# Three half chunks of a convolution's input gradient with leaf C by three products, twin sums in one instruction, and raw step buffers kept free of pair sums

## The chip, the core and the metric

The kernel runs on one core of one Trainium2 chip. The time is that of one launch on the device, in microseconds (us); the kernel before has three runs, and their median is what a new time is held against. One further execution was taken with the hardware profiler; every duration, wait and share below is of that execution. Its span goes from the first to the last recorded instruction.

## The reference, cut to what matters

A strided one-dimensional convolution (31 taps, stride 2, 256 channels to 256), a normalisation over time, a GELU, and the gradients of all of it.

```python
B, T, D, K = 2, 16000, 256, 31                      # x: (B, T, D), w: (K, D, D), all bf16
L = (T - K) // 2 + 1                                # 7985
h = sum(einsum('blc,cd->bld', x[:, i:i + 2*L:2, :], w[i]) for i in range(K))
h = (h - mean(h)) / sqrt(var(h) + 1e-5)             # over l, for each b and d
out = gelu(h * gn_gamma + gn_beta)
# returned: out, and the gradients of x, w, gn_gamma, gn_beta for a given grad_out (B, L, D)
```

The matmuls are those of three convolutions: the forward one, the one that gives the gradient of x, and the one that gives the gradient of w.

## The kernel before, in words

**Fewer products for sums.** Each convolution is split by even and odd positions, twice, and each split is done with three products in place of four: from the parts e0 and e1 of the data the kernel forms sums (the branches A, C and B of the first split, the leaves A, C and B of the second), multiplies each with a matching difference of weights, and adds the results with signs. A leaf can be done directly (helpers `f_leaf`, `g_leaf`, `w_leaf`) or split a third time. In the input gradient a direct leaf is 16 matmuls of 512 columns (`g_leaf`: two output parities, four positions, two channel halves). Split a third time it is 12: four by `g_three_b` or `g_outer` for the product that both parities share, and eight by `g_three_ac` on the sums of the two planes, which are formed by the function `third`. The shared product then has to be brought to both parities with opposite signs, which is work for VectorE (DVE) or ScalarE (ACT), in `g_seed`.

**Stages.** F0 and F1 are the forward pass of batch 0 and 1 (matmuls of line 596), G0 and G1 the input gradient (line 1162; G1 begins with the last chunk of batch 0), W the weight gradient (line 1447). GELU and its gradient (`gelu_unit`, lines 943 to 983) for batch 0 run beside F1, for batch 1 beside G0. The input gradient goes over two batches b, four chunks c, two half chunks pr, and the branches in the order B, A, C. In `input_grad` (line 1279) `GO` names the steps whose leaf A is split a third time (all of batch 1), and `GOC` the half chunks (b, c, pr) whose leaf C is too: the set is empty. Four PSUM tiles of two banks each are the ring in which a step's two results px and pt are built; before a leaf may add into its tile, `g_seed` (line 1202) must have written the signed results of the branch before into it, on DVE.

**Sums on DVE.** `third` and half of `second` add a plane to the other plane, and the other plane to the first one shifted by one element: always two instructions (lines 561 and 1121, through the local `tt`). In the weight gradient `pair_d` (line 1511) forms two differences of four rows each with two instructions at line 1516; `pair_x` (line 1504) is line 1508, `leaf_d` line 1587.

**The weight gradient's buffers.** `weight_grad` (line 1575) goes over nine steps n (`COMBOS`, line 22). For each, `x_tile` (line 1417) loads four blocks of x from HBM (1 MB each) into the tiles XS_ or XT_, by turns; where the step needs the sum of two raw blocks, the second is loaded into one of two raw buffers XR (byte 57344 and byte 65536 of the arena) and added by DVE (`w_add`, line 1413). Steps 2, 3, 5 and 6 need raw sums, the loads standing at the end of the step before. The pair sums of a step lie in sets named by `place` (line 1578): "all", "early" (steps 0 and 1) and "late", and the set "late" lies on the bytes of XR. Before, "late" is open to all steps but 3 and 5, by turns; step 4 puts the pair sums of its middle leaf there.

**The order.** Nothing of the order is written by hand. Each operation is recorded with an estimated duration; `Plan.order` (line 170) derives due times from the place of its readers among the matmuls, moved by a table of leads for each stage and kind of operation, and `Plan.listing` walks the engines and picks the most urgent ready operation. TensorE may take an operation up to `look` places ahead of the recorded order, and the result is pinned.

## Time and profile before

| what | value |
|---|---|
| runs | 1188.23, 1187.01, 1183.07 us; median 1187.01 us |
| profiled execution | 1189.54 us, of which the span is 1187.8 us |
| TensorE (PE) busy | 1149.0 us, 97% of the span |
| DVE busy | 1047.6 us, 88% |
| ACT busy | 570.0 us, 48% |
| granted TensorE clock, mean | 0.996 |
| forward matmuls (line 596) end | about 429 us |
| input gradient's matmuls (line 1162) | about 426 to 861 us |
| weight gradient's matmuls (line 1447) | about 861 us to the end |

The page of the profile gives, for each engine, busy time, and for each group of instructions "busy, mean ns of one | idle time of the engine before them and what ended it". [...] PEclk is the granted TensorE clock as a share of full speed.

### The profile page before, as it was taken

The numbers are of one execution on the slowest core, as the hardware profiler recorded it, in microseconds if no ns is written. First come the engines' busy times: TensorE is split into PE (matmuls) and PEld (weight loads), VectorE is DVE, ScalarE is ACT, GpSimd is POOL, SyncE is SP. The second block draws the span as 40 slices with busy tenths as digits, with TensorE's granted clock in tenths as the row PEclk, the third lists the DMA queues.
The fourth block names the chain that finished last, engine by engine and source line by source line (L and its number), as shares of the span: only waits on it lengthen the run. The fifth ranks groups of instructions, "written<-read, shape, count | busy, mean of one in ns | idle before, by whom it ended". The sixth has DMA issues, their size and how long they took to land.

```text
span 1187.8 us, 19338 instructions
## 1 busy us (share of the span) xinstructions
PE 1149.0 (97%) x7739; PEld 763.5 (64%) x7796; DVE 1047.6 (88%) x1358; ACT 570.0 (48%) x873; POOL 18.9 (2%) x67
## 2 busy tenths in 40 slices
PE   5999999999999999999999999999999999989998
PEld 3888889777777964444444444444488656656685
DVE  7997898799999989999879997788889898777995
ACT  1254454788885578978884476433322212111200
POOL 0000000000000000000000000000000000000000
PEclk9999999999999999999999999999999999999999
DMA  9446949968986799567639998697998824986774
GB/s 212 73 115 122 200 121 182 205 146 204 204 209 124 270 353 252 167 225 186 221 115 292 270 329 265 161 318 266 317 235 266 271 90 151 359 300 198 239 219 140
DMA packets 334100, 255.17 MB, mean 215 GB/s; under 512 B 187500, under 2 KB 312682, under 8 KB 325738
## 3 DMA queue, kind: packets, MB, share of 16 engines
q1 hardware_dynamic: 333818, 253.93, 76.6%
q8 instruction: 61, 1.00, 0.3%
q14 instruction: 29, 0.24, 0.1%
q0 software_dynamic: 192, 0.00, 0.0%
HBM read 118.95 MB, written 89.62 MB: 176 GB/s over the span
## 4 chain that ended last, share of the span: by engine, by line
PE 46%; DVE 14%; DMA 6%; issue 4%; ACT 1%; SPq 0%; DVEq 0%; ACTq 0%
PE ps L1162 27%; PE ps L1447 15%; PE ps L596 4%; DVE arena L1413 3%; DMA arena<-in_x_dram 2%; DMA arena<-dnd 2%; DVE arena L1357 2%; DVE arena L1587 2%; DVE ps L676 1%; DVE arena L676 1%; DVE arena L1516 1%; DVE arena L1508 1%; DMA dnd<-arena 1%; DVE arena L1121 1%; DVE ps L1540 1%
## 5 line engine op out<-in xcount | busy, mean ns | idle before, releaser
L1162 PE MATMUL ps<-arena 128*128 128x512 bf16 x1974 | 429.7, 376 | 6.6 <-DVE ps L676 3.6
L596 PE MATMUL ps<-arena 128*128 128x256 bf16 (+4 forms) x3460 | 408.2, 281 | 17.8 <-DVE arena L551 7.1
L596 PEld LDWEIGHTS <-arena 128*128 128x128 bf16 x3460 | 338.1, 99 | 87.7 <-DVE arena L551 7.5
L1162 PEld LDWEIGHTS <-arena 128*128 128x128 bf16 x2016 | 197.3, 98 | 237.7 <-issue 6.8
L1447 PE MATMUL ps<-arena 128*128 128x256 bf16 (+1 forms) x2305 | 312.1, 298 | 10.5 <-DVE arena L1508 7.3
L1447 PEld LDWEIGHTS <-arena 128*128 128x128 bf16 x2320 | 228.1, 98 | 94.6 <-DVE arena L1508 8.7
L691 ACT ACTIVATE arena<-ps 128x1024 f32<-128x1024 f32 (+1 forms) x143 | 145.7, 1020 | 285.3 <-PE ps L1447 98.1
L561 DVE TENSOR_TENSOR arena<-arena 128x1087 bf16<-128x1087 bf16 (+3 forms) x211 | 175.5, 866 | 13.7 <-PE ps L596 12.4
L968 DVE TENSOR_TENSOR arena<-arena 128x1024 bf16<-128x1024 bf16 x160 | 107.0, 683 | 8.5 <-ACT arena L962 3.9
L1413 DVE TENSOR_TENSOR arena<-arena 128x4096 bf16<-128x4096 bf16 x38 | 86.3, 2284 | 20.8 <-DMA arena<-in_x_dram 19.5
L1121 DVE TENSOR_TENSOR arena<-arena 128x516 bf16<-128x516 bf16 (+3 forms) x176 | 83.6, 506 | 8.6 <-PE ps L1162 8.0
L676 DVE TENSOR_TENSOR ps<-ps,arena 128x1024 f32<-128x1024 f32 x60 | 73.1, 1224 | 7.9 <-PE ps L1447 4.5
L1357 DVE TENSOR_TENSOR arena<-arena 128x768 bf16<-128x768 bf16 (+3 forms) x112 | 65.4, 636 | 9.9 <-DMA arena<-dnd 4.7
L711 ACT ACTIVATE arena<-ps 128x512 bf16<-128x512 f32 (+1 forms) x64 | 36.9, 578 | 70.4 <-PE ps L596 67.9
L676 DVE TENSOR_TENSOR ps<-arena,ps 128x1024 f32<-128x1024 f32 x44 | 53.8, 1223 | 9.3 <-PE ps L1162 5.5
L1532 ACT COPY ps<-ps 128x256 f32<-128x256 f32 x54 | 19.3, 357 | 78.7 <-PE ps L1447 77.6
L1587 DVE TENSOR_TENSOR arena<-arena 128x2304 bf16<-128x2304 bf16 x36 | 47.4, 1348 | 4.8 <-PE ps L1447 4.8
L1516 DVE TENSOR_TENSOR arena<-arena 128x1024 bf16<-128x1024 bf16 x76 | 48.7, 682 | 1.6 <-DMA arena<-d2d 1.6
L551 DVE TENSOR_TENSOR arena<-arena 128x2048 bf16<-128x2048 bf16 (+1 forms) x52 | 49.8, 989 | 0.0
L958 DVE SCALAR_TENSOR_TENSOR arena<-arena 128x1024 bf16<-128x1024 bf16 x32 | 39.0, 1219 | 11.3 <-ACT arena L956 11.1
L1189 ACT ACTIVATE ps<-ps 128x512 f32<-128x512 f32 x48 | 27.9, 582 | 41.1 <-PE ps L1162 38.0
L1508 DVE TENSOR_TENSOR arena<-arena 128x2048 bf16<-128x2048 bf16 x38 | 45.3, 1216 | 1.2 <-PE ps L1162 1.2
(79 smaller groups left out, 632.8 us busy)
## 6 DMA issues: line engine op xcount, KB each, us to landing
arena<-in_x_dram SPq DMA_DIRECT2D x40, 1024.0 KB, 9.8
arena<-d2d SPq DMA_DIRECT2D x16, 1216.0 KB, 11.5
out_dram<-arena SPq DMA_DIRECT2D x14, 1024.0 KB, 4.4
d2d<-arena SPq DMA_DIRECT2D x30, 384.0 KB, 7.1
arena<-dnd SPq DMA_DIRECT2D x10, 960.0 KB, 5.8
vl<-arena SPq DMA_DIRECT2D x36, 256.0 KB, 3.3
arena<-vl SPq DMA_DIRECT2D x9, 1024.0 KB, 6.8
hd<-arena SPq DMA_DIRECT2D x8, 1024.0 KB, 5.0
```

Source lines behind the costliest of these rows:

```text
L561: lambda: nc.vector.tensor_tensor(out=o, in0=a, in1=b, op=ALU.add))
L596: yield nc.tensor.matmul(ps[:, dh, cs], lhsT=wt, rhs=mv, start=s0, stop=False, skip_group_check=True)
L676: add("DVE", dve(1024, 1), [out], [a, b], lambda: nc.vector.tensor_tensor(out=out, in0=a, in1=b, op=op))
L691: lambda: nc.scalar.activation(out=out, in_=ps, func=ACT.Copy, scale=scale))
L968: add("DVE", dve(1024), [o], [a, b_], lambda: V.tensor_tensor(out=o, in0=a, in1=b_, op=op))
L1121: lambda: nc.vector.tensor_tensor(out=o, in0=a, in1=b, op=ALU.add))
L1162: yield nc.tensor.matmul(ps[:, e, 0:wide], lhsT=lt, rhs=mv, start=s0, stop=False, skip_group_check=True)
L1357: lambda: nc.vector.tensor_tensor(out=out, in0=a, in1=b_, op=ALU.subtract))
L1413: add("DVE", dve(4096), [o], [a, b], lambda: nc.vector.tensor_tensor(out=o, in0=a, in1=b, op=ALU.add))
L1447: yield nc.tensor.matmul(ps[:, s, c0:c1], lhsT=lt, rhs=mv, start=s0, stop=False, skip_group_check=True)
L1516: add("DVE", dve(1024), [d4[:, j]], [d], lambda j=j, o=o, st_=st_: nc.vector.tensor_tensor(out=d4[:, j], in0=d[:, o:o + 3 * st_ + 1:st_, : ...
L1587: add("DVE", dve(2304), [DL[i3, b]], [D2[b]], lambda b=b, i3=i3, o_=o_: nc.vector.tensor_tensor(out=DL[i3, b], in0=D2[b][:, o_:o_ + 17:2, ...
```

## The change

1. `GOC` is filled: leaf C of the half chunks (1, 1, 0), (1, 1, 1) and (1, 2, 0), three branches each, is split a third time. Its weight differences are formed by `w2_outer(C_)` before, and `third` runs once more for each of two chunks and three branches.
2. The two instructions of each twin sum become one. A helper `crossed` builds an access pattern whose first row is the other plane and whose second row is the first plane shifted by one element, that is, a row step of one element less than a plane, backwards. `pair_d` likewise becomes one instruction, with a negative row step. The pairs of sums in U and the last columns that are zeroed are laid out for it.
3. `place` closes the set "late" to steps 2 and 4 as well, so the raw buffers hold no pair sums from step 2 to step 5.
4. `f_first` records the first weight differences in another order, one of them after the first sum of x; `w2_part` of batch 0 is called at another branch in the first three chunks.
5. The planner's numbers are others: slack 50 in place of 70, `look` 14 in place of 13, the pads, the whole table of leads, and PACE, which spreads the GELU units.

```diff
-        self.look = 13
+        self.look = 14
...
-    U = [(sb(o, F), sb(o + 2176, F)) for o in (138240, 142592, 205312)]
+    U = [sb(o, 2, F) for o in (138240, 142592, 205312)]
...
         def third(lf, u):
             o = ops[lf]
-            tt(u[0], o[:, 0], o[:, 1], behind)
-            tt(u[1][:, 0:F - 1], o[:, 1, 0:F - 1], o[:, 0, 1:F], behind)
+            tt(u[:, :, 0:F - 1], o[:, :, 0:F - 1], crossed(o, F - 1), behind)
...
+    def crossed(v, n):
+        a = v[..., 1, 0:n]
+        dims = [list(x) for x in a.ap]
+        k = [list(x) for x in v.ap][-2][0]
+        return bass.AP(tensor=a.tensor, offset=a.offset, ap=dims[:-1] + [[1 - k, 2], [1, n]])
...
-                tt(l[:, 1, :, 0, 0:n], e1[:, :, 0, 0:n], e0[:, :, 1, 0:n])
-                tt(l[:, 1, :, 1, 0:n - 1], e1[:, :, 1, 0:n - 1], e0[:, :, 0, 1:n])
+                tt(l[:, 1, :, :, 0:n], e1[:, :, :, 0:n], crossed(e0, n))
...
-    GOC = set()
+    GOC = {(1, 1, 0), (1, 1, 1), (1, 2, 0)}
...
         d4 = p[1]
-        for j, o in ((0, o0), (1, o1)):
-            st_ = abs(o0 - o1)
-            add("DVE", dve(1024), [d4[:, j]], [d], lambda j=j, o=o, st_=st_: nc.vector.tensor_tensor(
-                out=d4[:, j], in0=d[:, o:o + 3 * st_ + 1:st_, :], in1=d[:, om:om + 3 * st_ + 1:st_, :], op=ALU.subtract))
+        k = abs(o0 - o1)
+        a, m = d[:, o0], d[:, om]
+        a = bass.AP(tensor=a.tensor, offset=a.offset, ap=[list(a.ap[0]), [-k * D, 2], [k * D, 4], [1, D]])
+        m = bass.AP(tensor=m.tensor, offset=m.offset, ap=[list(m.ap[0]), [0, 2], [k * D, 4], [1, D]])
+        add("DVE", dve(2048), [d4], [d], lambda: nc.vector.tensor_tensor(out=d4, in0=a, in1=m, op=ALU.subtract))
...
-            ks = ("all",) + (("early",) if n < 2 else ()) + (("late",) if n not in (3, 5) else ())
+            ks = ("all",) + (("early",) if n < 2 else ()) + (("late",) if n not in (2, 3, 4, 5) else ())
...
-    PACE = ((1385.0, 117.0), (191.0, 24.5))
+    PACE = ((1428.0, 62.5), (463.0, 25.0))
```

With `both` true in a step, the parts that were there already and now run are these (unchanged code):

```python
            g_outer(pt, br, planes(br, C_), o, C_)          # four matmuls of 512
...
            tc_ = GTC if br == A else [GRB[:, 1, e] for e in range(2)]
            for e in range(2):
                signed(tc_[e], e, pt[:, 1], GRB[:, 1, e])   # DVE, or ACT for branch B
            ve(vt, ts, vx, ALU.subtract)
            if br == A: half(px[:, e], px[:, e], tc_[e], ALU.add) for both e
            else:       ve(vx, vx, r1, ALU.add)
...
            g_three_ac(ps, br, C_, GUC[br], o)              # eight matmuls of 512, in place of g_leaf's 16
```

More of the change, by code (lines that the diff above doesn't have):

```diff
@@ new lines, in __init__ @@
+            "F0 f_evac last": -3.0,
+            "F0 f_mm f_outer": 2.0,
+            "F0 f_mm f_three_ac": -3.0,
+            "F0 f_mm f_three_b": 3.5,
+            "F0 f_outer forward": 9.0,
+            "F0 load put": -2.5,
+            "F0 tt second": 6.0,
+            "F0 turn w2_part": -5.0,
+            "F0 ve f_seed": -3.5,
+            "F0 w_sub w2_part": -0.5,
+            "F1 f_evac last": 3.0,
+            "F1 f_mm f_outer": -12.5,
+            "F1 f_mm f_three_ac": 4.0,
+            "F1 f_mm f_three_b": -6.5,
@@ new lines, in __init__ @@
+            "G0 zero gelu_batch": 4.0,
+            "G1 e_comp conv_stem_kernel": 9.0,
+            "G1 g_mm g_leaf": -5.0,
+            "G1 g_mm g_outer": 5.0,
+            "G1 g_mm g_three_ac": -3.5,
+            "G1 g_mm g_three_b": -1.0,
+            "G1 half g_seed": -4.0,
+            "G1 half signed": -7.0,
+            "G1 load d2_piece": 2.0,
+            "G1 load dn_turn": -12.0,
+            "G1 load e_load": -8.0,
+            "G1 load g_evac": 0.5,
+            "G1 signed g_seed": -9.0,
@@ new lines, in __init__ @@
+            "G1 sub d2_piece": -8.0,
+            "G1 tt first": -9.0,
+            "G1 tt second": 0.5,
+            "G1 tt third": 4.5,
+            "G1 turn dn_turn": 4.5,
+            "G1 ve g_seed": 5.5,
+            "G1 ve_neg g_seed": -8.0,
+            "G1 w_sub w2_outer": 7.0,
+            "G1 zero e_comp": -7.5,
+            "W keep w_keep": 10.0,
+            "W keep weight_grad": 8.0,
+            "W leaf_d weight_grad": -3.5,
+            "W load d_tile": 6.0,
+            "W load w_emit": 3.5,
```

161 lines of the change are left out of this document (69 added, 92 removed).

## The prediction

> **What bounds the kernel now.** I read the page's busy shares first, then the matmuls in order of time, then who waited for whom, then stages in windows.
>
> ```profile
> span 1187.8 us, 19338 instructions
> PE 1149.0 (97%) x7739; PEld 763.5 (64%) x7796; DVE 1047.6 (88%) x1358; ACT 570.0 (48%) x873; POOL 18.9 (2%) x67
> ```
>
> PE is busy for 1149.0 of 1187.8 us, so the kernel is bound by its matmuls, and only two things can shorten it: fewer matmul columns, or less of the 38.8 us in which PE stands still. DVE at 88% is the next engine: what is laid on it can come back as a wait of PE.
>
> ```profile
> PE ps L1447 <- DVE arena L1508: 7.3, 5, 4.2
> PE ps L596 <- DVE arena L551: 7.1, 2, 4.0
> PE ps L596 <- DMA arena<-in_x_dram: 5.8, 2, 4.7
> PE ps L1162 <- DVE ps L676: 3.6, 5, 1.3
> ```
>
> The columns are total, times, longest. The two L596 rows are the start of the kernel (first x, first weight differences). L1508 is `pair_x` of the weight gradient. L676 is the seeding of PSUM in the input gradient, only 3.6 us over all of it. The largest waits of the weight gradient, from PE's timeline:
>
> ```profile
> 974.40 0.61 PE L1447 MATMUL ps<-arena 128*128 128x256 bf16 x4 [1.72 <-DVE arena L1508]
> 975.53 41.41 PE L1447 MATMUL ps<-arena 128*128 128x256 bf16 x298 [0.53 <-DVE arena L1508]
> 1018.61 21.40 PE L1447 MATMUL ps<-arena 128*128 128x256 bf16 x130 [1.66 <-DVE ps L1540]
> 1044.18 16.20 PE L1447 MATMUL ps<-arena 128*128 128x256 bf16 x111 [4.17 <-DVE arena L1508]
> ```
>
> A stop also costs behind its end. The windows give length, busy time of each engine (count), then PEclk, the share of the DMA engines and GB/s:
>
> ```profile
> 975.00:979.00 4.00, 3.47 (x20) 2.50 (x20) 4.00 (x5) 0.26 (x1) 0.00 (x0) 0.63 0.92 276
> ...
> 1040.00:1044.00 4.00, 0.00 (x1) 0.00 (x0) 4.00 (x3) 0.63 (x1) 0.00 (x0) 1.00 1.00 314
> 1044.00:1048.00 4.00, 3.82 (x20) 2.73 (x21) 2.75 (x3) 0.99 (x3) 0.00 (x0) 0.57 1.08 358
> ```
>
> After the stop of 4.17 us the granted clock was 0.57 for 4 us: 4 x 0.43 = 1.7 us more, so that stop costs 5.9 us. After 1.72 and 0.53 us of standing still it was 0.63: 4 x 0.37 = 1.5 us, so that one costs 3.8 us.
>
> **The change part by part.** *Fewer matmuls.* Nine steps (three half chunks, three branches) exchange 16 matmuls of 512 columns for 12: 36 fewer, and the built program has exactly 36 fewer. Their pace, from stretches of the input gradient with almost no standing still:
>
> ```profile
> 706.00:732.00 26.00, 25.88 (x121) 11.80 (x121) 20.13 (x36) 16.51 (x23) 1.32 (x4) 1.00 1.08 311
> 732.00:758.00 26.00, 25.14 (x116) 11.39 (x117) 20.04 (x31) 18.21 (x24) 2.45 (x11) 1.00 0.72 184
> 758.00:784.00 26.00, 25.84 (x121) 11.89 (x122) 19.45 (x26) 8.86 (x11) 0.00 (x0) 1.00 0.67 217
> 784.00:810.00 26.00, 25.89 (x121) 11.90 (x122) 22.24 (x40) 8.86 (x11) 0.00 (x0) 1.00 0.84 283
> ```
>
> 25.89 / 121 = 0.214 us; 36 x 0.214 = **7.7 us** off PE. All of it is on the path, as PE is busy there almost without a break. Whether it stays won depends on DVE.
>
> *What the nine steps add.* Durations (mean ns of one):
>
> ```profile
> L676 DVE TENSOR_TENSOR ps<-ps,arena 128x1024 f32<-128x1024 f32 x60 | 73.1, 1224 | 7.9 <-PE ps L1447 4.5 <-ACT arena L691 3.4
> ...
> L561 DVE TENSOR_TENSOR arena<-arena 128x1088 bf16<-128x1088 bf16 x87 | 61.8, 717 | 7.9 <-PE ps L596 7.1 <-ACT arena L511 0.7
> L561 DVE TENSOR_TENSOR arena<-arena 128x1087 bf16<-128x1087 bf16 x85 | 60.7, 720 | 5.6 <-PE ps L596 5.3
> ...
> L1516 DVE TENSOR_TENSOR arena<-arena 128x1024 bf16<-128x1024 bf16 x76 | 48.7, 682 | 1.6 <-DMA arena<-d2d 1.6
> ...
> L1508 DVE TENSOR_TENSOR arena<-arena 128x2048 bf16<-128x2048 bf16 x38 | 45.3, 1216 | 1.2 <-PE ps L1162 1.2
> L561 DVE TENSOR_TENSOR arena<-arena 128x2176 bf16<-128x2176 bf16 x31 | 39.8, 1283 | 0.2
> ...
> L1121 DVE TENSOR_TENSOR arena<-arena 128x514 bf16<-128x514 bf16 x68 | 28.1, 422 | 0.9 <-PE ps L1162 0.9
> L1121 DVE TENSOR_TENSOR arena<-arena 128x516 bf16<-128x516 bf16 x68 | 27.6, 419 | 5.6 <-PE ps L1162 5.5
> ...
> L1121 DVE TENSOR_TENSOR arena<-arena 128x1036 bf16<-128x1036 bf16 x32 | 22.1, 690 | 2.1 <-PE ps L1162 1.6
> ...
> L683 DVE TENSOR_TENSOR arena<-ps,arena 128x512 f32<-128x512 f32 x16 | 10.9, 683 | 1.8 <-ACT arena L691 1.6
> ```
>
> On DVE: 18 instructions of 512 fp32 (branch A four more, branch C two more, per half chunk) at 0.683 = 12.3 us; the 1024-wide one that branch A saves is spent by branch B. Six more `third` at 0.690 = 4.1 us. Three weight differences of 2048 at 1.216 = 3.6 us. Together 20.0 us. On ACT six copies of 512, which its 48% share hides.
>
> Before, DVE works 20.13 + 20.04 + 19.45 = 59.6 of 78 us about where these half chunks lie. With 12.3 + 4.1 more it would be 76.0 us, against 78 - 7.7 = 70.3 us of matmuls. So DVE would fall behind by 5.7 us if nothing were moved. The built order does move work: of 28 differences of `d2_piece` that stand beside these half chunks 11 are left, the others stand earlier or later, where the weight gradient behind has room. The commonest of them:
>
> ```profile
> L1357 DVE TENSOR_TENSOR arena<-arena 128x768 bf16<-128x768 bf16 x60 | 30.2, 550 | 2.7 <-DMA d2d<-arena 2.7
> ```
>
> 17 x 0.55 = 9.4 us go, so DVE has 66.6 us of work beside 70.3: tight, and not over.
>
> *The waits that this adds.* A step of branch C now puts four 512-wide and two 1024-wide instructions in a row on DVE, 4 x 0.683 + 2 x 1.224 = 5.2 us, before both tiles are seeded. Queued behind them on DVE are the next chunk's sums. From the end of `g_three_ac` PE has eight matmuls of the last leaf C, four of the new outer product and four of the next step, 16 x 0.214 = 3.4 us. The wait is between nothing and 5.2 - 3.4 = 1.8 us a step, 0 to 16 us in nine. PE's look-ahead lets later leaves go first; the input gradient's usual wait is this one:
>
> ```profile
> 698.08 35.54 PE L1162 MATMUL ps<-arena 128*128 128x512 bf16 x161 [0.25 <-DVE ps L676]
> ```
>
> I take 0.25 us a step, **+2.3 us**.
>
> *Twin sums joined.* 85 pairs in the forward pass, 68 in the input gradient, 38 in `pair_d`: 191 instructions fewer. An isolated pair saves 0.717 + 0.720 - 1.283 = 0.15 us. Back to back, instructions overlap:
>
> ```profile
> 13.06 3.89 DVE L561 TENSOR_TENSOR arena<-arena 128x1087 bf16<-128x1087 bf16 x6
> 16.88 13.71 DVE L551 TENSOR_TENSOR arena<-arena 128x2048 bf16<-128x2048 bf16 x12
> ```
>
> (3.89 - 0.72) / 5 x 2 = 1.27 us a pair, against (13.71 - 1.22) / 11 = 1.14 us for 2048 elements, so 1.20 for 2174: 0.07 us. So DVE gets back 13 to 29 us over the kernel and pays 20.0: its total stays near 1048. Hardly any of this is on PE's path; at the start, three joins stand ahead of the fifth weight difference, for which PE waits: 3 x 0.07 = **0.2 us** off.
>
> *Raw buffers kept free.* In step 4 of the weight gradient the first pair sums lay on the raw buffers, so the raw blocks of step 5 could be loaded only when step 4's matmuls had read them:
>
> ```profile
> 950.00:1000.00 50.00, 47.59 (x305) 30.64 (x307) 49.95 (x43) 6.68 (x11) 0.00 (x0) 0.97 0.29 87
> 1000.00:1050.00 50.00, 44.06 (x310) 31.13 (x311) 35.92 (x27) 11.79 (x20) 0.00 (x0) 0.97 1.02 341
> ```
>
> ```profile
> 1015.12 2.29 DVE L1413 TENSOR_TENSOR arena<-arena 128x4096 bf16<-128x4096 bf16 x1 [9.38 <-DMA arena<-in_x_dram]
> ...
> 1023.02 4.62 DVE L1413 TENSOR_TENSOR arena<-arena 128x4096 bf16<-128x4096 bf16 x2 [3.34 <-DMA arena<-in_x_dram]
> ```
>
> The DMA engines stand nearly idle (0.29), then are full (1.02); DVE waits 9.38 and 3.34 us for raw blocks, and its late `pair_x` is what stops PE for 4.17 us. In the changed program's SyncE order two of the eight 1 MB loads of step 5 stand ahead of step 4's own loads of d, where the DMA engines are idle; 2 MB at 341 GB/s are 6.1 us less in the full stretch, more than 4.17. I take the whole stop: **-5.9 us**. The other bound: step 4's two sets of pair sums now share one set of buffers, as step 3's do already, and the stop at 974 us, at step 3's second set, cost 3.8 us. If step 4 gets the same, 5.9 - 3.8 = 2.1 us is left; if besides the old stop stays, it is 3.8 us worse. Against that, the built order sets two direct leaves, 16 matmuls of 512 columns each, between the parts of step 4's second set, about 2 x 16 x 0.214 = 6.8 us of cover.
>
> *The new order.* Leads, PACE and look-ahead move most instructions of every engine; work per stage stays. I price this at nothing, because outside the start and the weight gradient PE's waits are a few us in all; either sign of 4 us would not surprise.
>
> The sum: -7.7 + 2.3 - 0.2 - 5.9 = -11.5. The profiled execution took 1189.5 us (1.7 beside its span), so it becomes 1178.0; it stands 2.5 us above the median of the runs, and from the median the forecast is **1175.5 us**.
>
> **The rivals.**
>
> *The stop in the weight gradient stays, or moves to step 4's shared buffers.* For it: the burst of loads stays full, and step 3 shows such a stop. Against: the two early loads. 1175.5 + 5.9 = 1181.4, no change that counts.
>
> *DVE holds up the nine steps.* For it: 5.7 us too much work in place, and the chain of 5.2 us. Against: idle DVE before and after. All nine waits in full, 16 in place of 2.3: 1175.5 + 13.7 = 1189, no change.
>
> *The joined sums run slower* (the other side). Their second row starts at an odd element and lies before the first, an order that no instruction of the trace has. If this made them go one element at a time, as fp32 does ((1224 - 683) / 512 = 1.06 ns each), a sum of 2174 would take 2.44 us, 1.16 more; 85 of them are 98 us in the forward pass:
>
> ```profile
> 210.00:320.00 110.00, 109.83 (x834) 81.11 (x832) 100.04 (x151) 88.14 (x136) 0.23 (x1) 1.00 0.90 196
> 320.00:425.00 105.00, 103.72 (x869) 84.66 (x869) 104.56 (x149) 68.47 (x128) 3.57 (x11) 1.00 0.76 208
> ```
>
> DVE is full from 320 us on and has some 37 us free before 425 us, so some 60 us would come out, 1235 us. It decides from about (37 + 13) / 85 = 0.6 us more per sum. Against it: rows of 1087 and 257 elements that begin at an odd element run as fast as even ones (720 against 717 ns, 422 against 419). [...]
>
> **How the numbers follow.** Forecast 0.67; the stop stays 0.12; DVE holds up the steps 0.10; slower sums 0.07; the new order costs over 14 us in ways not listed 0.04. About 0.5% (5.9 us) is what a measurement tells from no change: faster 0.67, same 0.22, slower 0.11. The range goes down by what the forecast may gain beyond (step 3's stop gone too, 3.8, no waits in the nine steps, 2.3, and 3 for the order): 1166. It goes up past the two rivals without change, with 3 for the order: 1192.
>
> **What would show it.** Right: 36 matmuls fewer; joined sums of 2174 at about 1.28 us and of 1028 at 0.69; no PE stop over 2 us near the beginning of step 5, and no window there with a granted clock near 0.6; DMA share above 0.29 in the 50 us before it; waits for L676's successor in the input gradient under 6 us. Wrong: PE waits over 10 us in the three half chunks; a stop at step 4's second pair sums; joined sums over 1.9 us.

## The result and the profile after

The changed kernel is **slower**: 1198.72 us, median of four runs (1197.48 to 1199.78), against 1186.42 us for the kernel before, run beside it (four runs, 1183.07 to 1188.23). The ratio is 1.0108, 95% interval 1.0091 to 1.0125: 12.8 us lost where 11.5 were forecast to be won, and outside the range. The profiled execution took 1199.78 us with a span of 1198.0 us; its mean granted clock was 0.992, before 0.996.

The page's head of the changed kernel, in the form of the one shown of before:

```profile
span 1198.0 us, 19125 instructions
PE 1150.5 (96%) x7760; PEld 761.2 (64%) x7760; DVE 1052.6 (88%) x1194; ACT 574.3 (48%) x879; POOL 28.8 (2%) x67
```

The 36 matmuls are gone (weight loads: 7796 before, 7760 after), worth 7.7 us, and yet PE is busy 1.5 us longer, and stands still for 47.5 us where it stood still for 38.8. So about 9 us went into idle time and about 9 into slower busy time, and both together are more than the change removed. This split is rough: 57 matmul records of the kernel before are missing from its trace (7739 beside 7796 weight loads), so a part of its idle time may have been busy. The span is not touched by that.

Windows by stage say where. The first fence is the kernel before, the second the changed one; the rows are batch 1's forward pass (to the last forward matmul, rounded), then the two batches of the input gradient in two rows, then the weight gradient. Columns: length, busy time of PE, PEld, DVE, ACT and POOL with counts, then PEclk, DMA share, GB/s.

```profile
204.00:429.00 225.00, 222.49 (x1772) 172.77 (x1772) 214.60 (x316) 165.18 (x283) 3.80 (x11) 1.00 0.81 200
429.00:632.00 203.00, 202.00 (x937) 93.42 (x954) 181.38 (x286) 163.35 (x193) 6.35 (x20) 1.00 0.69 212
632.00:861.00 229.00, 223.54 (x1025) 102.18 (x1045) 197.26 (x308) 107.97 (x133) 4.71 (x23) 1.00 0.90 277
861.00:1187.80 326.80, 312.28 (x2307) 228.09 (x2320) 276.89 (x240) 55.02 (x89) 0.53 (x1) 0.99 0.74 224
```

```profile
202.00:439.00 237.00, 224.62 (x1765) 173.51 (x1764) 210.46 (x271) 164.21 (x278) 3.82 (x11) 0.99 0.74 184
439.00:655.00 216.00, 211.85 (x986) 96.75 (x985) 192.83 (x282) 172.58 (x206) 15.23 (x24) 0.99 0.73 222
655.00:885.00 230.00, 217.05 (x991) 97.17 (x990) 203.20 (x281) 104.64 (x132) 5.77 (x19) 0.99 0.82 261
885.00:1198.00 313.00, 308.69 (x2323) 226.97 (x2321) 273.77 (x203) 54.78 (x89) 0.53 (x1) 1.00 0.75 236
```

The forward pass of batch 1 went from 225.0 to 237.0 us, the input gradient from 432.0 to 446.0 in spite of the 36 matmuls, and the weight gradient from 326.8 to 313.0. The gain in the last stage came as forecast, and more than forecast; both stages ahead of it, for which the prediction had nothing and -7.7 + 2.3 us, lost about twice as much.

Who stopped PE in the changed kernel (total, times, longest):

```profile
PE ps L1184 <- DVE ps L700: 8.9, 12, 2.4
PE ps L613 <- ACT arena L735: 7.2, 3, 4.3
PE ps L613 <- DVE arena L571: 7.1, 2, 4.0
PE ps L613 <- DMA arena<-in_x_dram: 5.3, 2, 4.6
PE ps L613 <- ACT ps L649: 5.3, 4, 2.9
```

L613 is the forward pass's matmul, L1184 the input gradient's (596 and 1162 before), L700 the seeding on DVE. The two rows of the kernel's start (L571, in_x) are what they were. New among the large ones are the two rows of ScalarE: L735 is the evacuation of a finished PSUM tile, L649 the three copies that bring the shared product to its two places. The row of L1508, the largest of before with 7.3 us, is gone; the whole weight gradient has one stop of 0.3 us left.

PE's timeline (start, length of the stretch without a stop, count, and the wait before it) at the large stops:

```profile
261.56 24.09 PE L613 MATMUL ps<-arena 128*128 128x512 bf16 x164 [4.26 <-ACT arena L735]
288.58 11.64 PE L613 MATMUL ps<-arena 128*128 128x256 bf16 x74 [2.93 <-ACT ps L649]
...
327.67 22.42 PE L613 MATMUL ps<-arena 128*128 128x512 bf16 x164 [2.79 <-ACT arena L735]
```

```profile
686.30 34.39 PE L1184 MATMUL ps<-arena 128*128 128x512 bf16 x160 [1.77 <-DVE ps L700]
721.43 10.67 PE L1184 MATMUL ps<-arena 128*128 128x512 bf16 x48 [0.74 <-DVE ps L700]
732.30 3.61 PE L1184 MATMUL ps<-arena 128*128 128x512 bf16 x16 [0.19 <-DVE ps L700]
...
878.50 7.03 PE L1184 MATMUL ps<-arena 128*128 128x512 bf16 x24 [2.36 <-DVE ps L700]
```

The forward pass has three large stops, and one of 1.54 us at 351.63. The input gradient has many small ones: between 439 and 885 us they are 25 and make 17.0 us, where before there were 7 and 4.4. Here a short stop cost more than its idle time: in the stretch of 160 matmuls one takes 34.39 / 160 = 0.215 us, so 16 are 3.44 us, but the 16 between two stops kept PE "busy" for 3.61 (so at 732.30, and again at 680.91 and 872.53). That is 0.17 us a stop; for 18 more stops I estimate some 3 us. The granted clock, 0.99 in the two rows of the input gradient where it was 1.00, fell at two places, behind the stops of 0.92 us at 459.69 and of 2.36 us at 878.50:

```profile
459.60:463.60 4.00, 3.91 (x11) 1.48 (x11) 4.00 (x5) 3.61 (x6) 0.94 (x3) 0.57 1.13 368
...
879.00:883.00 4.00, 4.00 (x13) 1.48 (x12) 4.00 (x5) 1.02 (x1) 0.00 (x0) 0.58 0.98 316
```

By the clock I estimate that at 4 x 0.43 + 4 x 0.42 = 3.4 us. The windows of 22 to 30 us between 640 and 848 us all show 1.00, with most of the 25 stops in them, so a slow clock does not follow every stop.

**Where the loss of the forward pass begins.** There one can follow a chain by hand. First VectorE's timeline of the changed kernel, then ScalarE's, then SyncE's queue:

```profile
245.37 1.29 DVE L581 TENSOR_TENSOR arena<-arena 128x2174 bf16<-128x2174 bf16 x1 [4.44 <-DMA arena<-in_x_dram]
246.57 1.28 DVE L993 TENSOR_TENSOR arena<-arena 128x1024 bf16<-128x1024 bf16 x2
```

```profile
247.29 1.06 ACT L1003 ACTIVATE arena<-arena 128x1024 bf16<-128x1024 bf16 x1 [4.13 <-DVE arena L993]
248.25 0.19 ACT L1003 ACTIVATION_READ_ACCUMULATOR arena<-arena 128x1 f32 x1
248.35 0.58 ACT L735 ACTIVATE arena<-ps 128x512 bf16<-128x512 f32 x1
...
260.84 0.57 ACT L735 ACTIVATE arena<-ps 128x512 bf16<-128x512 f32 x1
```

```profile
232.12 3.65 SPq L440 DMA_TRANSPOSE arena<-arena  x2
238.65 0.33 SPq L435 DMA_DIRECT2D arena<-hd  x1
239.03 4.10 SPq L440 DMA_TRANSPOSE arena<-in_x_dram  x1
```

From the end of the chain: SyncE issues the x load at 239 us, behind GELU's two transposes and GELU's load of hd, which wait for GELU's work on VectorE. So VectorE's joined sum waits 4.44 us for x; the GELU product behind it on VectorE (L993) is late; ScalarE's activation L1003 waits 4.13 us for that; and the evacuation L735, which has nothing to do with x or GELU, stands behind L1003. In this way a late DMA of one kind can reach PE through three queues, each worked off in its order, with waits of 4.44, 4.13 and 4.26 us here. The trace does not show the whole way: the evacuation that ends PE's stop is the last row, at 260.84, 12 us later, with other activations of GELU before it. At 288 us, in the same way, the three copies L649 lie one by one between GELU activations.

### The profile page after: what moved, and what is told of

It is laid out like the page before. It is cut to its first block, busy times and chain, and to the rows that moved or that the text cites. A ratio compares the mean times of both kernels' runs of the same rounds, so it can differ in the third digit from the quotient of the medians.

```text
span 1198.0 us, 19125 instructions
## 1 busy us (share of the span) xinstructions
PE 1150.5 (96%) x7760; PEld 761.2 (64%) x7760; DVE 1052.6 (88%) x1194; ACT 574.3 (48%) x879; POOL 28.8 (2%) x67
## 4 chain that ended last, share of the span: by engine, by line
PE 65%; DVE 17%; DMA 7%; ACT 7%; issue 4%; SPq 1%; DVEq 0%; ACTq 0%
PE ps L613 24%; PE ps L1469 23%; PE ps L1184 17%; DVE arena L1379 4%; DMA arena<-dnd 3%; DVE ps L700 3%; DMA d2d<-arena 2%; DVE arena L581 2%; DVE arena L571 1%; DVE arena L707 1%; DMA arena<-in_x_dram 1%; DVE arena L1146 1%; ACT arena L735 1%; ACT arena L981 1%; DVE arena L1096 1%
## 5 line engine op out<-in xcount | busy, mean ns | idle before, releaser
L1184 PE MATMUL ps<-arena 128*128 128x512 bf16 (+1 forms) x1980 | 430.8, 378 | 17.1 <-DVE ps L700 8.9
L613 PE MATMUL ps<-arena 128*128 128x256 bf16 (+4 forms) x3460 | 412.0, 282 | 26.1 <-ACT arena L735 7.2
L613 PEld LDWEIGHTS <-arena 128*128 128x128 bf16 x3460 | 339.6, 99 | 98.4 <-issue 18.1
L1184 PEld LDWEIGHTS <-arena 128*128 128x128 bf16 x1980 | 194.6, 98 | 252.4 <-issue 30.3
L1469 PE MATMUL ps<-arena 128*128 128x256 bf16 (+1 forms) x2320 | 308.3, 296 | 0.3 <-DVE ps L700 0.3
L715 ACT ACTIVATE arena<-ps 128x1024 f32<-128x1024 f32 (+1 forms) x143 | 145.8, 1022 | 304.3 <-PE ps L1184 122.3
L581 DVE TENSOR_TENSOR arena<-arena 128x2174 bf16<-128x2174 bf16 (+3 forms) x126 | 167.6, 1350 | 33.6 <-PE ps L613 25.6
L993 DVE TENSOR_TENSOR arena<-arena 128x1024 bf16<-128x1024 bf16 x160 | 107.7, 685 | 13.7 <-ACT arena L985 7.2
L1146 DVE TENSOR_TENSOR arena<-arena 128x1028 bf16<-128x1028 bf16 (+3 forms) x114 | 80.3, 729 | 13.1 <-PE ps L1184 8.7
L1379 DVE TENSOR_TENSOR arena<-arena 128x768 bf16<-128x768 bf16 (+3 forms) x112 | 66.6, 636 | 11.5 <-DMA arena<-dnd 7.8
L700 DVE TENSOR_TENSOR ps<-ps,arena 128x1024 f32<-128x1024 f32 x60 | 73.1, 1224 | 3.9 <-PE ps L1469 3.9
L735 ACT ACTIVATE arena<-ps 128x512 bf16<-128x512 f32 (+1 forms) x64 | 37.1, 583 | 76.5 <-PE ps L613 73.5
L700 DVE TENSOR_TENSOR ps<-arena,ps 128x1024 f32<-128x1024 f32 x44 | 53.8, 1222 | 3.8 <-PE ps L613 2.8
L571 DVE TENSOR_TENSOR arena<-arena 128x2048 bf16<-128x2048 bf16 (+1 forms) x55 | 53.9, 1002 | 0.1
L1540 DVE TENSOR_TENSOR arena<-arena 128x2048 bf16<-128x2048 bf16 x38 | 45.2, 1215 | 6.3 <-PE ps L1469 4.2
L1530 DVE TENSOR_TENSOR arena<-arena 128x2048 bf16<-128x2048 bf16 x38 | 45.4, 1216 | 1.5 <-PE ps L1184 1.4
L649 ACT ACTIVATE ps<-ps 128x256 f32<-128x256 f32 x75 | 27.6, 368 | 36.7 <-PE ps L613 35.3
## 6 DMA issues: line engine op xcount, KB each, us to landing
arena<-d2d SPq DMA_DIRECT2D x16, 1216.0 KB, 11.5
```

Of the source, the lines that this page charges most:

```text
L571: add("DVE", dve(n), [o], [a, b, *then], lambda: nc.vector.tensor_tensor(out=o, in0=a, in1=b, op=ALU.subtract))
L581: lambda: nc.vector.tensor_tensor(out=o, in0=a, in1=b, op=ALU.add))
L613: yield nc.tensor.matmul(ps[:, dh, cs], lhsT=wt, rhs=mv, start=s0, stop=False, skip_group_check=True)
L700: add("DVE", dve(1024, 1), [out], [a, b], lambda: nc.vector.tensor_tensor(out=out, in0=a, in1=b, op=op))
L715: lambda: nc.scalar.activation(out=out, in_=ps, func=ACT.Copy, scale=scale))
L735: lambda o=o, i=i, ac=ac: nc.scalar.activation(out=o, in_=i, func=ACT.Copy, accum_out=ac))
```

## The experiments

Theory at the outset: the parts are sound, and the loss is in the **order** that the planner makes when the recorded operations and its numbers change. Rivals: a part itself costs time (the joined sums, or the three products, keep VectorE from its work); or one of the planner's numbers does it. The fourth item of the change has no run of its own. In the code `w2_part` of batch 0 moves to another branch in the last chunk alone (`A if c == 3 else C_`), not in the first three as the list of the change says; and the two rows of the kernel's start, where the differences of `f_first` stand, are what they were.

### The parts against the planner's numbers

`new_parts_old_numbers` is the changed kernel with slack, look, pads, leads and PACE of before; `old_parts_new_numbers` is the opposite: parts as before, planner's numbers of after; `no_third_leaf_c` is the changed kernel with the set emptied.

```diff
# new_parts_old_numbers
-        self.slack = 50.0
+        self.slack = 70.0
...
-        self.look = 14
+        self.look = 13
...
-    PACE = ((1428.0, 62.5), (463.0, 25.0))
+    PACE = ((1385.0, 117.0), (191.0, 24.5))
# no_third_leaf_c
-    GOC = {(1, 1, 0), (1, 1, 1), (1, 2, 0)}
+    GOC = set()
```

> All new parts (leaf C of three half chunks by three products, joined sums, raw buffers kept free) with the planner's numbers of before (slack, look, pads, leads, PACE). Order theory: the loss comes from the new planner's numbers, so the parts alone gain: 7.7 us less PE work and the stop of step 5 gone, 1174 to 1182 us. Parts theory: the nine three-product steps cost more DVE and ACT time than they save, so this stays at 1195 us or more. If numbers of before do not fit the new parts, new waits of PE would show in F1 or G1.

> The kernel before with the planner's numbers of after. Order theory: it loses by itself, 1195 to 1210 us, with ACT-ended waits of PE (evacuation of the forward PSUM, line 711) of 3 to 4 us each between 250 and 350 us as in the changed kernel. Parts theory: within 5 us of before, 1182 to 1192 us.

> The changed kernel with no half chunk's leaf C by three products (36 matmuls more). Parts theory: the loss of some 11 us between the half chunk (1, 1, 0) and the weight gradient goes, 1188 to 1194 us. Order theory: the three products do gain there, so without them it is as slow as the changed kernel or slower, 1198 to 1207 us.

Measured: 1226.98 us (ratio 1.0339, 1.0315 to 1.0363), 1204.64 us (1.0159, 1.0131 to 1.0186) and 1201.61 us (1.0124, 1.0104 to 1.0145). Each half of the change is slower alone than the whole. The first is far from the 1174 to 1182 us of the order theory, the other two lie in its ranges. The second is the plainest test of the order: it is the kernel before with other planner's numbers, and its counts are those of before (7796 weight loads, 1358 instructions on DVE, 873 on ACT):

```profile
PE 1153.1 (96%) x7796; PEld 763.8 (64%) x7796; DVE 1047.2 (87%) x1358; ACT 569.0 (47%) x873; POOL 23.0 (2%) x67
```

The same instructions in another order take 1.59% longer, 18.9 us (14.3 by the profiled spans, 1187.8 to 1202.1), though its waits for the evacuations on ScalarE are 2.5 and 2.4 us, not 3 to 4. With the old numbers (PE's timeline of the first kernel) the loss sits in batch 1's input gradient:

```profile
739.51 3.60 PE L1164 MATMUL ps<-arena 128*128 128x512 bf16 x8 [10.29 <-DVE arena L551]
...
894.25 3.57 PE L1164 MATMUL ps<-arena 128*128 128x512 bf16 x8 [7.15 <-DVE ps L680]
```

and the forward pass loses hardly anything; with the new numbers the forward pass loses even without the new parts. So the new numbers are in part a repair of what the parts do to the order, and they bring a loss of their own. Without the three products the changed kernel is 0.16% slower, 1.9 us, with intervals that overlap; the profiled spans say 4.5 us (1202.5 against 1198.0). Neither is a gain of the stage itself. These are PE's rows for the input gradient (busy, mean of one, idle), with the three products and without:

```profile
L1184 PE MATMUL ps<-arena 128*128 128x512 bf16 (+1 forms) x1980 | 430.8, 378 | 17.1 <-DVE ps L700 8.9
```

```profile
L1184 PE MATMUL ps<-arena 128*128 128x512 bf16 (+1 forms) x2016 | 435.7, 378 | 12.0 <-DVE ps L700 4.3
```

The mean of one, 378 ns, is longer than busy time over count, 430.8 / 1980 = 0.218 us, as the records overlap in the trace. 430.8 + 17.1 = 447.9 us against 435.7 + 12.0 = 447.7: what the 36 matmuls save is given back in stops, and the 4.5 us lie in the other two stages, whose order moved. So nothing is won by this part in the changed kernel, and taking it out does not give the loss back.

### Each part alone with the planner's numbers of before

`only_raw_free` is the kernel before with one line changed; `raw_free_joined` has the joined sums besides, recorded as joined; `raw_free_third_c` has the filled set besides, without joins.

```diff
-            ks = ("all",) + (("early",) if n < 2 else ()) + (("late",) if n not in (3, 5) else ())
+            ks = ("all",) + (("early",) if n < 2 else ()) + (("late",) if n not in (2, 3, 4, 5) else ())
# raw_free_joined, besides: the joined forms of the change, among them
-            tt(u[0], o[:, 0], o[:, 1], behind)
-            tt(u[1][:, 0:F - 1], o[:, 1, 0:F - 1], o[:, 0, 1:F], behind)
+            tt(u[:, :, 0:F - 1], o[:, :, 0:F - 1], crossed(o, F - 1), behind)
# raw_free_third_c, besides
-    GOC = set()
+    GOC = {(1, 1, 0), (1, 1, 1), (1, 2, 0)}
```

> The kernel before with nothing changed but the set of pair buffers on the raw buffers closed to steps 2 and 4. The weight gradient was 14 us shorter in the changed kernel. If the raw buffers did that, this gives 1172 to 1180 us and a weight gradient of 312 to 320 us in place of 326.8; if the joined pair differences or the new leads did it, within 3 us of before.

> The kernel before, its planner's numbers kept, with the raw buffers kept free and the twin sums joined; no three products for leaf C. If a joined sum costs what its elements say, DVE gets back 13 to 29 us and this is as fast as the raw buffers alone or up to 4 us faster, 1175 to 1181 us. If joining costs (a longer instruction holds the engine, both rows wait for the later of their inputs, or the old numbers do not fit), 1185 us or more.

> The kernel before, its numbers kept, with the raw buffers kept free and leaf C of the three half chunks by three products; no sums joined. If the three products gain as forecast, 1180 less some 5 us, 1173 to 1177 us. If their place costs (weight differences that wait for buffers, signed copies on a full DVE), one or more waits of PE over 5 us between 650 and 780 us and 1185 to 1215 us.

Measured: **1180.05 us** (0.9937, 0.992 to 0.9955); 1207.65 us (1.0165, 1.0141 to 1.019); 1225.25 us (1.0323, 1.0306 to 1.0339).

The raw buffers alone win 0.63%. Their windows at the place where the prediction showed those of before:

```profile
950.00:1000.00 50.00, 47.08 (x313) 30.20 (x312) 50.00 (x42) 7.26 (x11) 0.00 (x0) 1.00 0.42 130
1000.00:1050.00 50.00, 50.00 (x376) 36.61 (x375) 40.33 (x32) 11.46 (x19) 0.00 (x0) 1.00 1.03 354
```

The DMA engines work at 0.42 in the first 50 us (0.29 before), and in the second PE never stops (44.06 us busy before, clock 0.97). The stages ahead stay: the weight gradient's matmuls begin at 862.12 us, before at 861.19. Joined sums or three products on top, however, lose 28 and 45 us against it. In the kernel with three products the two largest stops are these:

```profile
734.82 3.59 PE L1162 MATMUL ps<-arena 128*128 128x512 bf16 x8 [10.58 <-DVE arena L551]
...
893.77 10.45 PE L1162 MATMUL ps<-arena 128*128 128x512 bf16 x40 [9.26 <-DVE ps L676]
```

L551 are the weight differences of leaf C. In VectorE's queue they stand behind differences of `d2_piece` (L1357). One of these waited 7.2 us for something that the profile doesn't name, and earlier ones up to 1.3 us for DMAs through DRAM; that such round trips hold up the 7.2 us too is read, not shown.

### Joined in place: the same instructions, the order kept

If the joined instructions cost nothing themselves, they must be free when the order is kept. `joined_in_place` is `only_raw_free` whose order is planned with the separate sums; then each pair is merged where one of the two can take over the other's place without passing a reader or a writer. 189 instructions go from VectorE (1358 to 1169).

```diff
+        for a, b, fn in self.twins:
+            a, b = sorted((a, b), key=place.get)
+            if all(place[q] < place[a] for q in self.ops[b]["preds"] if q != a):
+                self.ops[a]["fn"] = fn
+                gone.add(b)
+            elif all(place[q] > place[b] for q in after.get(a, ()) if q != b):
+                self.ops[b]["fn"] = fn
+                gone.add(a)
```

> The kernel before with the raw buffers kept free, and its order worked out from the separate sums; only then each pair of sums that can be is put into one instruction, at the place of one of the two. So the joining is there and the reordering that it causes in the planner is not. If the joined instruction itself costs (holds DVE longer, waits for the later input), 1195 to 1208 us as where the planner saw the joined sums. If the reordering cost those 27 us, 1176 to 1182 us, as the raw buffers alone or a little faster.

Measured: **1178.71 us** (0.9936, 0.9911 to 0.996). The two kernels `raw_free_joined` and `joined_in_place` have the same parts and the same planner's numbers; one is 1.65% slower than before, the other 0.64% faster. What differs is the order, beside two of the 191 pairs that stay separate, and it is worth 27 us. Against `only_raw_free` (0.9937) the joins give nothing that can be measured. This is the version that beats both kernels, together with `only_raw_free`.

Merging in place also let the three products be tried at one half chunk, with the order planned for them: `one_half_chunk`.

```diff
-    GOC = set()
+    GOC = {(1, 2, 0)}
...
-        if (b, c, pr, br) == (1, 0, 1, A) and GOC:
+        if (b, c, pr, br) == (1, 1, 1, B_) and GOC:
```

> As the sums joined in place with free raw buffers, with leaf C by three products in one half chunk alone, (1, 2, 0), its weight differences formed one half chunk before it and not at (1, 0, 1): 12 matmuls fewer, 2.6 us of PE. If the stop of 10.6 us for these differences came from the d2 pieces whose bytes they take, it is gone here and this gives 1 to 3 us less than the sums joined in place; if three products on a full DVE cost, more than that kernel.

Measured: 1203.01 us (1.0137, 1.0114 to 1.0161). The 10 us stop for the weight differences is gone, as their call is later; yet 12 matmuls fewer cost 24 us against `joined_in_place`, 9 of them in one stop some 75 us behind the half chunk, where seeds (L710) stand on VectorE behind work for the weight gradient:

```profile
842.60 22.35 PE L1202 MATMUL ps<-arena 128*128 128x512 bf16 x96 [1.96 <-DVE ps L710]
873.99 10.54 PE L1202 MATMUL ps<-arena 128*128 128x512 bf16 x40 [9.03 <-DVE ps L710]
```

### Single numbers of the planner

```diff
# before_look14
-        self.look = 13
+        self.look = 14
# before_slack50
-        self.slack = 70.0
+        self.slack = 50.0
# after_old_pace
-    PACE = ((1428.0, 62.5), (463.0, 25.0))
+    PACE = ((1385.0, 117.0), (191.0, 24.5))
# after_old_forward, besides the forward pass's leads (30 entries for 27)
-    PACE = ((1428.0, 62.5), (463.0, 25.0))
+    PACE = ((1385.0, 117.0), (463.0, 25.0))
```

> The kernel before with one planner's number of the change, look 14 in place of 13. PE's order alone changes at a few dozen places, no work. If the order is a close fit, so that any departure costs, 1192 us or more; else within 4 us of before.

> The kernel before with one planner's number of the change, slack 50 in place of 70: DVE, ACT and SyncE change places, PE hardly. If the order is a close fit, 1192 us or more; else within 4 us of before.

> The changed kernel with the spread of the GELU units of before (PACE alone). If the spread of GELU's work put it ahead of the PSUM evacuations on ACT between 250 and 350 us, the waits of PE for ACT there go and this gives 1183 to 1190 us. If the table of leads did it, 1195 us or more, and the waits stay.

> The changed kernel with the leads of the two forward stages and the spread of GELU's first batch from before; slack, look-ahead and pads stay new. If the order of the second forward half costs the 15 us between 255 and 430 us, this gives 1183 to 1188 us. If slack, look-ahead and pads did it, 1195 us or more.

The kernel before with look 14 in place of 13: 1186.41 us (1.0005, 0.9993 to 1.0017). With slack 50 in place of 70: 1187.5 us (1.0000, 0.9987 to 1.0012). The changed kernel with PACE of before: 1200.07 us (1.0109, 1.0089 to 1.013). The changed kernel with the forward pass's leads and first PACE pair of before: 1219.51 us (1.0278, 1.0259 to 1.0297). Three of the four do nothing, so it isn't true that any other number of the planner costs time. In `after_old_pace` the waits for ScalarE stay too (7.2 and 5.3 us). With the parts of the change, half of the older table in the newer one (1219.51 us) lies between the whole newer one (1198.72) and the whole older one (1226.98).

### Which places in the queues

The trace shows urgent work behind background work, so the first idea was to put all of it ahead. `evac_first` re-sorts ScalarE's queue in batch 1's forward pass, `seed_first` VectorE's in batch 1's input gradient and in the weight gradient, `both_first` does both, and `half_chunk_seed_first` does the second in `one_half_chunk`.

```diff
+        todo = self.front(todo, "ACT", lambda o: o["kind"].split()[0] == "F1" and o["ps"],
+            lambda o: "gelu" in o["kind"] or (o["kind"].split()[0] == "F1" and not o["ps"]), 6)
...
+        todo = self.front(todo, "DVE", lambda o: o["kind"].split()[0] in ("G1", "W") and o["ps"],
+            lambda o: "d2_piece" in o["kind"] or "x_tile" in o["kind"] or "weight_grad" in o["kind"] and not o["ps"], 8)
```

> The changed kernel, with ScalarE's queue alone re-sorted in the forward pass of batch 1: an operation that reads or writes PSUM goes up to six places ahead of GELU work and of work without PSUM that stood before it, where no data forbids it; matmuls keep their order. Theory (the evacuations stand behind GELU activations that wait for VectorE): TensorE's waits of 4.3 and 2.8 us for ScalarE around 260 and 328 us go, the pass is 7 to 12 us shorter, and the kernel takes 1187 to 1192 us. Rival (VectorE is late for its loads, and whatever it feeds is late in any order): the waits take another name, and the time is within 3 us of the changed kernel's 1198.7.

> The changed kernel, with VectorE's queue alone re-sorted in batch 1's input gradient and in the weight gradient: an operation that reads or writes PSUM goes up to eight places ahead of differences for the weight gradient, sums of its x blocks and its pair sums. Theory (the seeds stand behind background work): the waits of 1.8 and 2.4 us for VectorE at 686 and 878 us go and G1 is 4 to 8 us shorter: 1191 to 1195 us. Rival (VectorE is simply full there): within 3 us of 1198.7, the waits moved to the matmuls that need the differences.

> Both re-sortings in the changed kernel. Theory: the gains add, 1181 to 1187 us, no slower than the kernel before. Rival (late loads or a full VectorE): within 3 us of 1198.7.

> The kernel one_half_chunk (order planned with separate sums, pairs joined in place, raw buffers free, one half chunk by three products: 1203.0 us) with VectorE's queue re-sorted as in seed_first. Theory: the 9.0 us stop at 874 us and the stops of 2 us around it were seeds behind background work, and go: 1180 to 1190 us. Rival: the stop was the lateness of the loads that VectorE's x sum waited for, and it stays: 1200 or more.

Measured: 1229.21 us (1.0332, 1.0303 to 1.0361), 1297.86 (1.0914, 1.0888 to 1.0941), 1327.1 (1.1173, 1.1147 to 1.1198) and 1314.75 (1.1063, 1.104 to 1.1086). Both theory and rival fell: all four are far slower. The longest waits of VectorE and of PE in `seed_first` say why there:

```profile
DVE ps L1587 <- PE ps L1493: 45.4, 16, 12.4
```

```profile
PE ps L1493 <- DVE arena L1554: 39.3, 10, 12.1
```

VectorE's operations on PSUM, put ahead, stand at the head of its queue and wait for matmuls that aren't done, 45.4 us at one line; behind them stands `pair_x` (L1554 there), and the matmuls wait for it. In `evac_first` the forward pass lost some 28 us, with PE waiting for VectorE's weight differences (12.7 us at once); its way there was not followed. "Works on PSUM" is not "urgent": what counts is whether its input is there when its turn comes.

So the last two runs moved only what has nothing new to wait for. `x_turns_together` moves the second to fourth x load of a chunk, which wait for the same readers of the old buffer as the first, at most three places ahead past GELU's DMAs; `x_turns_and_copies` besides moves the later copies L649 of a tile, and the second evacuation of a tile, at most two places ahead.

```diff
+        todo = self.front(todo, "SP", lambda o: o["up"] > 0, lambda o: "gelu" in o["kind"] or "out0_store" in o["kind"], 3)
...
+        todo = self.front(todo, "ACT", lambda o: o["up"] > 0, lambda o: "gelu" in o["kind"] or "f_evac" in o["kind"] and not o["ps"], 2)
```

> The changed kernel, with the second to fourth x load of each chunk of batch 1's forward pass moved at most three places ahead in SyncE's queue, past GELU's DMAs; six of twelve loads move, matmuls keep their order. Theory (VectorE's 4.4 us at 241 us, and with it ScalarE's 4.1 us and TensorE's 4.3 us at 257 us, come from the fourth load standing behind GELU's DMAs): those waits go, the pass is 4 to 7 us shorter, 1192 to 1195 us. Rival (the DMA engines were full there, and the load would land as late in any place of the queue): within 2 us of 1198.7.

> As x_turns_together, and in ScalarE's queue of the same pass the three copies that one tile of the shared product needs, and the two evacuations of one tile, are at most two places closer together, past GELU activations and squares. Theory: the waits of 2.9, 2.8 and 1.5 us for ScalarE at 286, 325 and 350 us shrink by 1 to 2 us each: 3 to 5 us below x_turns_together, 1188 to 1191 us. Rival (a later evacuation at the head of the queue waits for its matmuls and holds GELU up, as in evac_first): no better than x_turns_together, or worse.

Measured: 1197.47 us (1.0103, 1.0086 to 1.012) and 1193.8 us (1.0064, 1.0045 to 1.0083), against 1.0108 for the changed kernel. VectorE's wait of 4.44 us and ScalarE's of 4.13 us are gone in the first. PE's stop behind them shrank, but not to nothing; this is its timeline in the first kernel, then in the second:

```profile
259.63 22.41 PE L644 MATMUL ps<-arena 128*128 128x512 bf16 x164 [2.41 <-ACT arena L766]
284.98 21.03 PE L644 MATMUL ps<-arena 128*128 128x256 bf16 x144 [2.94 <-ACT ps L680]
...
324.90 22.41 PE L644 MATMUL ps<-arena 128*128 128x512 bf16 x164 [2.79 <-ACT arena L766]
```

```profile
259.33 22.42 PE L655 MATMUL ps<-arena 128*128 128x512 bf16 x164 [2.55 <-ACT arena L777]
282.85 15.88 PE L655 MATMUL ps<-arena 128*128 128x256 bf16 x120 [1.11 <-ACT ps L691]
299.20 3.65 PE L655 MATMUL ps<-arena 128*128 128x512 bf16 x24 [0.46 <-ACT arena L777]
...
321.56 22.41 PE L655 MATMUL ps<-arena 128*128 128x512 bf16 x164 [2.65 <-ACT arena L777]
```

The last forward matmul ends at 438.9 us in the changed kernel, 436.1 in the first and 432.5 in the second (429.1 before). By the spans the first step is worth 2.7 us (1198.0 to 1195.3), and the second 4.7 more (1190.6). By the runs the first gives 0.05%, which is inside the uncertainty and what its rival said, and both together 0.44%, 5.2 us. So the places of the copies and evacuations are shown to cost time. Of the 3.6 us of the forward pass 1.8 are shorter stops (from 200 us on they make 10.8 us, then 9.0); of the rest, 1.5 us lie in the 144 matmuls behind the second stop, which take 21.03 us in the first kernel and 15.88 + 3.65 = 19.53 in the second. Whether the granted clock did that was not shown for this stretch; over the whole execution it was 0.994 and 0.997. The late x load is shown to make VectorE and ScalarE wait, and only a part of PE's stop hangs on it.

## Why the prediction was wrong

**What bounds the kernel.** Right as a reading of before. Wrong in what was taken from it: that PE's waits were few in the old order was used as evidence on the new one.

**Fewer matmuls, -7.7.** The count is right and the pace (0.215 us) too; that all of it is on the path did not hold. With the 36 matmuls put back, and the order planned anew, PE's busy time in the stage is 4.9 us longer and its idle time 5.1 us shorter, so none of the 7.7 us arrives in the stage.

**The waits of the nine steps, +2.3.** From 719 to 800 us, where the three half chunks begin and end, the changed kernel has 11 stops of together 4.1 us. That is 1.8 us more than priced, the stops' tails of 0.17 us not counted. Only half of it is the mechanism that was named: 2.1 us end with VectorE's work on PSUM (L700, L707), and 2.0 us with evacuations on ScalarE (L715), which the prediction took to be hidden by ScalarE's 48% share. The rival "DVE holds up the nine steps" (16 us in all) did not come there, but one of the signs of being right failed: L700's waits over the whole input gradient were to stay under 6 us and are 8.9.

**Twin sums joined.** Right for the single sum. By form in the changed kernel:

```profile
L581 DVE TENSOR_TENSOR arena<-arena 128x2174 bf16<-128x2174 bf16 x85 | 108.7, 1289 | 31.8 <-PE ps L613 24.9 <-DMA arena<-in_x_dram 6.5
...
L1146 DVE TENSOR_TENSOR arena<-arena 128x1028 bf16<-128x1028 bf16 x42 | 28.5, 692 | 6.8 <-ACT arena L1106 3.6 <-PE ps L1184 3.1
```

1289 and 692 ns where 1.28 us and 0.69 were asked for. The rival of 2.44 us a sum falls. What DVE gets back was put too high, 13 to 29 us: 189 joins in place bring its busy time from 1047.5 us (`only_raw_free`) to 1036.6, 10.9 us.

**Raw buffers kept free, -5.9.** Right, mechanism and place; the size was larger. Alone it wins 0.63%, 7.5 us, or 8.9 us by the profiled spans (1187.8 to 1178.8). PE now runs through step 5 and the feared stop at step 4's second set did not come:

```profile
974.97 0.61 PE L1447 MATMUL ps<-arena 128*128 128x256 bf16 x4 [2.40 <-DVE arena L1508]
976.10 112.63 PE L1447 MATMUL ps<-arena 128*128 128x256 bf16 x780 [0.52 <-DVE arena L1508]
```

Two stops of before are gone, the 4.17 us that were priced and the 1.66 us at 1018.61 that were not, together 5.8 us. The clock of 0.97 in both 50 us windows is 1.00, by which I estimate another 3 us (100 x 0.03). A part of that is luck, as far as the runs tell: step 3's stop is still there, 2.40 us in place of 1.72, and the slow clock that stood behind it before is not. In the changed kernel the weight gradient is 13.8 us shorter, as step 3's stop is gone too.

**The new order, 0, "either sign of 4 us".** This is the step that failed: "I price this at nothing, because outside the start and the weight gradient PE's waits are a few us in all." The chance given to more than 14 us from this was 0.04. The runs show what stands in its place: the instructions of before with the new planner's numbers alone take 18.9 us more (`old_parts_new_numbers` at 1.0159), and two orders of the joined sums differ by 27 us (`raw_free_joined` at 1.0165 of before, `joined_in_place` at 0.9936). In the changed kernel the raw buffers are worth 7.5 to 8.9 us by their run alone and the three products 0 to 4.5, and the span is 10.2 us longer: what is left for the new order, by subtraction, is 18 to 24 us. At the end of the forward pass 9.8 us of it are to be seen. The small waits of before were no property of the stage but of one order: the same instructions in `old_parts_new_numbers` stop PE for 4.0 us at once in the input gradient and for 8.8 us in the weight gradient, for a load of x.

**What is shown and what is not.** Shown: an order alone costs more than the whole loss, with the instructions unchanged; the raw buffers are a gain and the joins are neutral in the order of `only_raw_free`; taking the three products out of the changed kernel gives nothing back; places in ScalarE's queue cost part of the forward pass's loss. That the order is the whole loss of the changed kernel is got by subtraction. Only read from traces: the chain from the x load over VectorE and ScalarE to PE as the cause of the whole stop at 257 us; moving the load took away the waits on the way, and left 2.4 of 4.3 us. Open: which places cause the 14 us of the input gradient, where 12.6 us more of idle time lie in 25 small stops, and whether the three products can be had at their full 7.7 us in any order. Every order that was tried with them in the input gradient of before lost more than they give.

## What to carry to other kernels

Where a scheduler makes the order, an edit to what it schedules is a new order for the queue of every engine, and "the waits are small now" is no bound for what that costs; give it a range on both sides, and expect the loss side. To keep a local gain, keep the order: change one line that moves a buffer, or merge instructions in the places they already have. Of the re-sorts here only those that put ahead what had nothing new to wait for did no harm, and the two together gave 5.2 us; moving a class of work ahead because its readers are urgent made VectorE's queue wait at its head (45.4 us at one line in `seed_first`).

## What the runs showed of the hardware

In the changed kernel a two-row operand whose second row starts one element less than a plane before the first ran in 1289 ns for 2174 elements in bf16 (L581, 85 times), and a plain operand of 2176 in 1284 ns (the same line, 31 times). So the negative step, here in the outer dimension, went with 5 ns more.

GpSimd's small copies (L1123) became slower without having been changed. In the kernel before and in the changed one:

```profile
L1098 POOL COPY arena<-arena 128x12 bf16<-128x12 bf16 x12 | 3.7, 310 | 163.8 <-ACT arena L1081 81.7 <-issue 81.6 <-DVE arena L968 0.5
```

```profile
L1123 POOL COPY arena<-arena 128x12 bf16<-128x12 bf16 x12 | 10.8, 907 | 165.9 <-issue 83.9 <-ACT arena L1106 82.0
```

In the kernel `joined_in_place`, with its joined sums, they take 314 ns, so it isn't the joins by themselves; what stands beside them in the changed order wasn't tried, and each figure is of one profiled execution.
